# Loading K and V of two heads per transfer in a one-token attention kernel

## The chip, the cores and the metric

The kernel runs on one core of a Trainium2 chip. The metric is the device time of one execution in microseconds. Three timed executions of the kernel before took 524.91, 525.25 and 526.60 us; their median, 525.25 us, is the number that the changed kernel is measured against. The engines are called by their short names: PE is TensorE (PEld its weight loads), DVE is VectorE, ACT is ScalarE, POOL is GpSimd, SP is the engine that issues the DMAs here.

## What is computed

One token passes through two attention layers and two small mixer layers, in turn, with the same weights and the same K and V caches both times:

```python
x = A_x                                                   # (1, 1, 640)
x = x + _A_ref(_layernorm(x), A_k_cache, A_v_cache, A_wq, A_wo)
x = x + _B_ref(_layernorm(x), B_w1, B_w2, B_w3, B_w4)
x = x + _A_ref(_layernorm(x), A_k_cache, A_v_cache, A_wq, A_wo)
x = x + _B_ref(_layernorm(x), B_w1, B_w2, B_w3, B_w4)

def _A_ref(x, k_cache, v_cache, wq, wo):                  # 32 heads, Dh = 192
    W = 4096                                              # the last 4096 of 32768 keys
    q = (x @ wq) split into heads
    k, v = k_cache[:, :, Sk - W:, :], v_cache[:, :, Sk - W:, :]
    p = softmax(einsum("bhqd,bhkd->bhqk", q, k) * Dh ** -0.5)
    return (einsum("bhqk,bhkd->bhqd", p, v) joined over heads) @ wo
```

`_B_ref` is a layer norm, a gelu MLP of 640 to 1536 to 640, and a residual. (A part of it multiplies rows shifted in time; with one row it adds nothing, and the kernel leaves it out.) One head's K is 4096 x 192 bf16 numbers, 1.573 MB, and so is its V. Read twice for 32 heads, K and V make up nearly all the data that the kernel moves.

## The kernel before

**Data and cells.** K of a head lies in HBM as 4096 rows of 192 numbers. One DMA (`load_k`, L130) puts it into a cell of on-chip memory: partition p of the 128 gets keys 32p to 32p + 31, which are 12,288 contiguous bytes. V is loaded in the same way (`load_v`, L143). There are 11 cells of 12,288 bytes per partition (`NCELL`, L74). `take` (L114) hands out the cell that has been free longest, `give` (L119) returns it. Weights wo, w3 and w4 live in cells too. K of seven heads (`NKEEP`) stays on chip in transposed form between the two attention layers; two V heads and a part of a third are kept as well.

**The order of loads.** `layer_stream` (L203 on) writes down the order of all loads for a layer, and `need` issues them in that order on SP as the program asks for them. The instructions themselves may run long before: SP issues a load as soon as its cell is free, and a limited number of loads may be in flight. All engines but POOL run in the order in which the program was written (`manual_schedule`).

**Scores.** The matmul needs the 192 head dimensions on partitions. `transpose_quart` (L358) turns a quarter of a head's K with one DVE transpose in blocks of 32 x 32 words of 4 bytes (L375, 768 words per partition), four times a head. The target is a cell called the area, one head large, whose quarters are reused in turn. `scores` (L441) then runs 24 matmuls a head (L451, 256 columns each) for one head; the head's query stands in `Qblk` in a block form. Scores of four heads share one PSUM tile.

**Softmax.** Heads are treated in eight groups of four. `softmax_steps` (L471) has the steps part_max (DVE, L476), turn_max (PE, L481), full_max (DVE, L486 and L491), spread_max (PE L499, then ACT's exp, L505), turn_p (DVE, L510), swap (16 small PE matmuls with the constant `Eq`, L521, and an ACT copy to `PT`, L524), recip.

**PV and the fold.** `pv` (L558) multiplies a head's probabilities with V in 16 matmuls of 384 columns (L567): two key rows at once, a weight of two columns. The sum is in `O_ps`, of which there is one. A DVE transpose (L574) brings it to `o_sb`; `o_fold` (L576) sums it over partitions with small matmuls. `out_proj` or `out_row` multiply with wo.

**The order of work in a group.** The loop at L732 works on group `cur` while it prepares the scores of the next, `nxt`. It first runs the softmax of `cur`, interleaved with the transposes and scores of the first head of `nxt` (L764 to L799). Then for each head of `cur` it runs `pv`, then the transposes and scores of another head of `nxt` (L838 to L842), then `o_fold`. In the last two groups (`hurry`, `final`) the scores are pulled forward and the softmax of the last group is run early. Layer 0 goes through the groups from head 31 down to 0, layer 1 from 0 up.

**The end.** After the last V come wo of the last two groups in pieces, w3 and w4 in halves; the mixer of layer 1 works on each as it lands (L860 on), and a row of 640 numbers is stored.

Of the kernel before, what the change touches and what calls it, by code (L numbers as in the profile page):

```python
# [17 lines left out]
P = 128  # L18
# [17 lines left out]
def kernel(  # L36
# [26 lines left out]
    QH = 4  # L63
# [12 lines left out]
    NKEEP, NCELL = 7, 11  # L76
# [13 lines left out]
    cells = ctx.enter_context(tc.tile_pool(name="cells", bufs=1))  # L90
# [15 lines left out]
    kx = const.tile([P, VN], BF16, name="kx")  # L106

# [3 lines left out]
    free = deque(range(NCELL))  # L111
    cell_of = {}

    def take(key):  # L114
        i = free.popleft()
        cell_of[key] = i
        return cells.tile([P, FREE], BF16, tag=f"cell{i}", name=f"cell{i}")

    def give(key):  # L119
        free.append(cell_of.pop(key))  # L120
# [11 lines left out]

    def load_v(layer, h):
        t = take(("v", layer, h))
        src = A_v_cache[0, h, s0:Sk, :].rearrange("(p j) d -> p (j d)", p=P)
        cut = (2 * VW,) if h == VP else (FREE - VN,) if h == VX else ()
        if layer == 1 and h in GROUPS[layer][-1][-2:]:
            cut = FREE // 2,
        i = 0
        for e in cut + (FREE,):  # L140
            kept_v = h == VP or h == VX and i > 0
            if layer == 0 or not kept_v:
                nc.sync.dma_start(v_pair(t, h, i, e - i), src[:, i:e])  # L143
            i = e
        return t
# [55 lines left out]
    LOADERS = {"x": load_x, "k": load_k, "v": load_v, "wq": load_wq, "wo": load_wo, "w3": load_w3, "w4": load_w4}  # L201

    def layer_stream(layer):  # L203
# [14 lines left out]

        if layer == 0:
            for hh in groups[0]:  # L220
                k_item(hh)
        for gi, cur in enumerate(groups):
            nxt = list(groups[gi + 1]) if gi + 1 < len(groups) else []
            late = gi + 2 >= len(groups)
            for i, hh in enumerate(cur):
                if nxt:
                    k_item(nxt.pop(0))
                if nxt and late and i == 2:
                    k_item(nxt.pop(0))
                v_item(hh)  # L230
                if later and seq[-1] == ("k", layer, NKEEP):
                    seq.append(later.pop())
                if layer == 0 and gi + 1 == len(groups) and i < 2:
                    seq.append(("wo", layer, groups[gi + i - 1][0] // QH))
            if gi + 2 < len(groups) and gi >= layer:
                seq.append(("wo", layer, cur[0] // QH))
# [25 lines left out]
    ones = const.tile([P, P], F32, name="ones")  # L262
    nc.vector.memset(ones[:], 1.0)
# [13 lines left out]
    even = const.tile([P, 1], F32, name="even")  # L277
    nc.vector.reduce_sum(even[:], ident[:].rearrange("p (m two) -> p m two", two=2)[:, :, 0], axis=AX.X)
    lo = const.tile([P, 1], F32, name="lo")
    nc.vector.reduce_sum(lo[:], ident[:, 0:64], axis=AX.X)  # L280
    maskq = const.tile([P, 4], F32, name="maskq")
    nc.vector.tensor_tensor(out=maskq[:, 0:1], in0=lo[:], in1=even[:], op=ALU.mult)
    nc.vector.tensor_tensor(out=maskq[:, 1:2], in0=lo[:], in1=maskq[:, 0:1], op=ALU.subtract)
    nc.vector.tensor_tensor(out=maskq[:, 2:3], in0=even[:], in1=maskq[:, 0:1], op=ALU.subtract)
    nc.vector.tensor_scalar(out=maskq[:, 3:4], in0=lo[:], scalar1=-1.0, scalar2=1.0, op0=ALU.mult, op1=ALU.add)
# [6 lines left out]
    eps1 = const.tile([P, 1], F32, name="eps1")  # L292
    nc.vector.memset(eps1[:], eps)
# [26 lines left out]
    def ln_center(x, rowsum):  # L320

        mean_ps = psm.tile([P, 1], F32, tag="psm")
        nc.tensor.matmul(mean_ps[:], lhsT=ones[:], rhs=rowsum[:, 0:1], start=True, stop=True)
# [10 lines left out]
        def total():  # L334
            var_ps = psm.tile([P, 1], F32, tag="psm")
            nc.tensor.matmul(var_ps[:], lhsT=ones[:], rhs=ssq[:, 0:1], start=True, stop=True)
            return var_ps
# [20 lines left out]
    def transpose_quart(layer, h, q):  # L358
# [17 lines left out]
        if q == NT - 1:  # L376
            give(("k", layer, h))
        return T
# [62 lines left out]
    def scores(h, Ts, q0, ST_ps, hq):  # L441

        ng = NGK // NT
        Q = Qblk[:, h // QH % 2, hq * QHEAD:(hq + 1) * QHEAD].rearrange("p (f x) -> p f x", x=QW)
        views = [T.rearrange("p (g f i t) -> p g f i t", f=NFB, g=ng, i=P) for T in Ts]
        for f in range(NFB):
            for t in range(2):
                n = 2 * f + t
                for i, T4 in enumerate(views):
                    r = 32 * (q0 + i)  # L450
                    nc.tensor.matmul(  # L451
                        ST_ps[r:r + QW, :].rearrange("p (g i) -> p g i", g=ng), lhsT=Q[:, n, :],
                        rhs=T4[:, :, f, :, t],
                        start=(hq == 0 and n == 0), stop=(hq == QH - 1 and n == NCOL - 1))
# [16 lines left out]
    def softmax_steps(n, ST_ps, sc):  # L471
# [25 lines left out]
        def spread_max():  # L497
            nb_ps = psm.tile([P, 1], F32, tag="psm")
            nc.tensor.matmul(nb_ps[:], lhsT=held["w"],  # L499
                             rhs=ones[0:1, 0:1], start=True, stop=True)  # L500
# [13 lines left out]

        def swap():
            ng = NGK // NT
# [6 lines left out]
            PT = big.tile([P, n, NJ4 * NGK], BF16, name="PT")  # L523
            nc.scalar.copy(PT[:].rearrange("p h c -> p (h c)"), PT_ps[:].rearrange("p h j g -> p (h j g)"))  # L524
            l_ps = psm.tile([P, QH], F32, tag="psm")
            nc.tensor.matmul(l_ps[:], lhsT=ones[:], rhs=held["lh"][:], start=True, stop=True)  # L526
            held["lps"] = l_ps
            return PT
# [28 lines left out]

    def pv(layer, h, hq, PT, mid=None):  # L558
# [17 lines left out]
    def o_fold(h, oT, rl, add=False):  # L576
        r = slice(32 * (h % QH), 32 * (h % QH) + 32)
        oT_ps = psm.tile([P, NA], F32, tag="psm")
        if not add:
            for e in range(2):  # L580
                nc.tensor.matmul(oT_ps[r, :], lhsT=Lq[:], rhs=o_sb[:, e, :, e], start=(e == 0), stop=(e == 1))  # L581
# [3 lines left out]
        nc.vector.tensor_add(o2[:], o_sb[:, 0, :, 0], o_sb[:, 1, :, 1])  # L585
# [53 lines left out]
    def attention(layer, x_cur, rs_cur, x_new, z_new, rs_new, ss_new):  # L639
# [5 lines left out]
        last_plain = [h for g in groups for h in g if h >= NKEEP][-1]  # L645
# [3 lines left out]
        def softmax_scale():  # L649
            rstd = power(total()[:, 0:1], 1.0 / D, eps1[:], "rstd")  # L650
# [6 lines left out]

        def S(h, half, ST_ps, hq):
            if layer == 1 and h < NKEEP:
                if half == 1:  # L660
                    scores(h, [Th.pop((h, q)) for q in range(NT)], 0, ST_ps, hq)
                    give(("T", h))
                return
            scores(h, [Th.pop((h, q)) for q in (2 * half, 2 * half + 1)], 2 * half, ST_ps, hq)
            if half == 1 and layer == 0 and h == last_plain:
                give(("area", layer))
                area[0] = None

        def add_y(y_ps, n):
            y_new = x_new if n == 0 else sm.tile([P, ND], F32, name="y_acc")  # L670
            if n == 1:
# [5 lines left out]
                def center():  # L677
                    nm_ps = psm.tile([P, 1], F32, tag="psm")
                    nc.tensor.matmul(nm_ps[:], lhsT=ones[:], rhs=rs[:, 0:1], start=True, stop=True)
# [25 lines left out]
        for hq, h in enumerate(groups[0]):  # L705
            for half in range(2):
                if layer == 0:
                    T(h, half)
                else:
                    Th.update({(h, q): transpose_quart(layer, h, q) for q in (2 * half, 2 * half + 1)})  # L710
                S(h, half, ST, hq)
                if (hq, half) == (0, layer):
                    qb[2]()
                    qb[3]()
# [17 lines left out]
        for gi, cur in enumerate(groups):  # L732
            nxt = list(enumerate(groups[gi + 1])) if gi + 1 < len(groups) else []
            ST_n = None
            if nxt:
                part_max, turn_max, full_max, spread_max, turn_p, swap, recip = softmax_steps(len(cur), ST, sc)
                ST_n = next_scores()
                if layer == 1 and gi == 0:
# [7 lines left out]
                    for q2, h2 in keep:  # L746
                        for half in range(2):
                            T(h2, half)
                            S(h2, half, ST_n, q2)
# [10 lines left out]
                else:  # L760
# [3 lines left out]
                    h0 = nxt[0][1]  # L764
                    T(h0, 0)
                    part_max()
                    T(h0, 1)
                    S(h0, 0, ST_n, 0)
                    turn_max()
                    full_max()  # L770
                    S(h0, 1, ST_n, 0)
                    spread_max()
                    h1 = nxt[1][1]
# [9 lines left out]
                    T(h1, 0)  # L783
# [12 lines left out]
                    T(h1, 1)  # L796
# [3 lines left out]
                    nxt.pop(0)  # L800
# [7 lines left out]
            if layer == 1 and gi == 0:  # L808
                order.insert(0, order.pop(cur.index(VC)))
            for hq, h in order:  # L810
                pv(layer, h, hq, PT, fold)
                if final:
# [5 lines left out]
                    if hq < QH - 2:  # L818
                        o_fold(h, oT, rl)
                    else:  # L820
                        def fold(h=h):
                            o_fold(h, oT, rl)

                    continue
                if hurry and hq == 1:
                    (q2, h2), (q3, h3) = nxt
                    for half in range(2):
                        T(h2, half)
                        S(h2, half, ST_n, q2)
                    T(h3, 0)  # L830
                    S(h3, 0, ST_n, q3)
                    T(h3, 1)
                elif hurry and hq == 2:
                    S(h3, 1, ST_n, q3)
                    steps = softmax_steps(len(cur), ST_n, sc)
                    steps[0]()
                    steps[1]()
                elif nxt and not (hurry and hq == 3):  # L838
                    q2, h2 = nxt.pop(0)
                    for half in range(2):  # L840
                        T(h2, half)
                        S(h2, half, ST_n, q2)  # L842
                o_fold(h, oT, rl, len(groups) - 4 > gi >= 2 * layer)
# [14 lines left out]
    def mixer(layer, x_cur, z, rs_cur, ss_cur, x_new, rs_new):  # L858
# [5 lines left out]
        nc.tensor.matmul(s1_ps[:], lhsT=ones[:], rhs=rs_cur[:, 0:1], start=True, stop=True)  # L864
        s2_ps = psm.tile([P, 1], F32, tag="psm")
        nc.tensor.matmul(s2_ps[:], lhsT=ones[:], rhs=ss_cur[:, 0:1], start=True, stop=True)
# [119 lines left out]
```

## Time and profile before

| What | Value |
|---|---|
| median of three runs | 525.25 us |
| the profiled execution: span from first to last instruction | 522.9 us |
| its own time beyond the span | not given |
| HBM read | 216.47 MB, 414 GB/s over the span |
| PE busy | 330.3 us (63%), 4146 matmuls |
| DVE busy | 294.6 us (56%), 589 instructions |
| ACT busy | 49.5 us (9%) |
| mean granted TensorE clock | 0.675 of full |
| one K or V load | 1536 KB; in steady state 26 to 31 us from issue to landing, since several wait in the queue |

Some groups of instructions, by shape:

```profile
L574 DVE STREAM_TRANSPOSE o_sb<-O_ps 128x384 f32<-128x384 f32 x64 | 37.2, 582 | 112.4 <-PE O_ps L567 112.3
...
L375 DVE STREAM_TRANSPOSE cell_277<-cell_1403 128x768 uint32<-128x768 uint32 x4 | 3.7, 956 | 0.1
```

Each row names the line, the engine and operation, output and input with shapes and count; then busy us and mean ns of one; then how long the engine stood idle just before, and for whom. A busy share is an average over the whole run. The rows of the page that show the DMA engines, and the chain of waits, are in the prediction; both say what happens where, which a busy share doesn't.

### The profile page before, as it was taken

The numbers are of one execution on the slowest core, as the hardware profiler recorded it, in microseconds if no ns is written. First come the engines' busy times: TensorE is split into PE (matmuls) and PEld (weight loads), VectorE is DVE, ScalarE is ACT, GpSimd is POOL, SyncE is SP. The second block draws the span as 40 slices with busy tenths as digits, with TensorE's granted clock in tenths as the row PEclk, the third lists the DMA queues.
The fourth block names the chain that finished last, engine by engine and source line by source line (L and its number), as shares of the span: only waits on it lengthen the run. The fifth ranks groups of instructions, "written<-read, shape, count | busy, mean of one in ns | idle before, by whom it ended". The sixth has DMA issues, their size and how long they took to land.

```text
span 522.9 us, 9589 instructions
## 1 busy us (share of the span) xinstructions
PE 330.3 (63%) x4146; PEld 195.5 (37%) x4146; DVE 294.6 (56%) x589; ACT 49.5 (9%) x175; POOL 4.0 (1%) x16
## 2 busy tenths in 40 slices
PE   2057668666665566767655866667675666647675
PEld 2023334333332333434333544334343333425344
DVE  2067656666574664556624264766576866654722
ACT  1000101010010100001011101001010101001011
POOL 2000000000000000000000000000000000000000
PEclk9995656567677776576555567657787865766755
DMA  8999999999999999999999999999999999999996
GB/s 345 429 424 425 423 426 427 423 424 423 427 421 428 424 422 428 423 423 423 423 399 398 388 425 427 424 424 423 426 423 424 426 423 426 421 427 425 420 410 237
DMA packets 23949, 217.08 MB, mean 415 GB/s; under 512 B 2532, under 2 KB 3044, under 8 KB 8420
## 3 DMA queue, kind: packets, MB, share of 16 engines
q1 hardware_dynamic: 23908, 216.48, 99.0%
q8 instruction: 32, 0.52, 0.4%
q14 instruction: 9, 0.07, 0.0%
HBM read 216.47 MB, written 0.00 MB: 414 GB/s over the span
## 4 chain that ended last, share of the span: by engine, by line
DMA 43%; PE 27%; DVE 25%; issue 2%; ACT 2%; SPq 1%; DVEq 0%; ACTq 0%
PE ST_ps L451 11%; DVE cell_3304 L375 9%; PE O_ps L567 8%; DVE cell_277 L375 8%; DMA cell_1925<-in_A_k_cache_dram 6%; DMA cell_4933<-in_A_k_cache_dram 5%; DMA cell_1629<-in_A_k_cache_dram 5%; DMA cell_1329<-in_A_k_cache_dram 5%; DMA cell_4637<-in_A_k_cache_dram 5%; DMA cell_5324<-in_A_v_cache_dram 5%; DMA cell_275<-in_A_k_cache_dram 4%; DVE o_sb L574 2%; DMA cell_2478<-in_A_v_cache_dram 2%; DMA cell_2690<-in_A_v_cache_dram 2%; DMA cell_5423<-in_B_w_dram 2%
## 5 line engine op out<-in xcount | busy, mean ns | idle before, releaser
L451 PEld LDWEIGHTS <-Qblk 128*16 128x16 bf16 x1536 | 86.1, 113 | 178.6 <-issue 151.1
L451 PE MATMUL ST_ps<-cell_277,Qblk 128*16 128x256 bf16 x600 | 70.1, 392 | 50.9 <-DVE cell_277 L375 34.3
L574 DVE STREAM_TRANSPOSE o_sb<-O_ps 128x384 f32<-128x384 f32 x64 | 37.2, 582 | 112.4 <-PE O_ps L567 112.3
L451 PE MATMUL ST_ps<-cell_3304,Qblk 128*16 128x256 bf16 x600 | 67.3, 382 | 43.5 <-DVE cell_3304 L375 28.3
L567 PEld LDWEIGHTS <-PT 128*2 128x2 bf16 x1024 | 47.2, 102 | 21.8 <-issue 11.3
L510 DVE STREAM_TRANSPOSE o_sb<-o_sb 128x256 bf16<-128x256 bf16 x16 | 7.1, 445 | 34.1 <-ACT o_sb L505 25.0
L582 ACT ACTIVATE oT<-oT_ps,rl 32x6 bf16<-32x6 f32 x40 | 10.3, 258 | 163.5 <-PE oT_ps L581 157.1
L581 PEld LDWEIGHTS oT_ps<-o_sb,Lq 128*32 128x32 f32 x160 | 13.2, 145 | 19.9 <-issue 16.1
L581 PE MATMUL oT_ps<-o_sb,Lq 128*32 128x6 f32 x160 | 13.9, 196 | 10.4 <-DVE o_sb L574 9.9
L587 ACT ACTIVATE oT<-oT_ps,rl 32x6 bf16<-32x6 f32 x24 | 6.2, 258 | 108.4 <-PE ST_ps L451 93.7
L405 PE MATMUL qT_ps<-xc,wq_sb 128*128 128x1 bf16 x210 | 7.2, 165 | 13.4 <-DMA wq_sb<-in_A_wq_dram 12.5
L419 DVE TENSOR_TENSOR Xq<-qT_ps,maskq 128x24 bf16<-128x24 f32 (+1 forms) x18 | 2.8, 157 | 18.3 <-PE qT_ps L405 18.3
L521 PE MATMUL PT_ps<-o_sb,Eq 128*32 128x32 bf16 x256 | 7.2, 237 | 9.2 <-DVE o_sb L510 4.0
L394 PE MATMUL qr_ps<-wq_sb,xc 128*1 128x384 bf16 x90 | 12.8, 433 | 0.0
L521 PEld LDWEIGHTS <-Eq 128*32 128x32 bf16 x256 | 5.5, 111 | 18.9 <-issue 18.8
L405 PEld LDWEIGHTS <-wq_sb 128*128 128x128 bf16 x210 | 6.8, 104 | 14.8 <-DMA wq_sb<-in_A_wq_dram 13.6
L502 ACT COPY nb_sb<-nb_ps 128x1 f32<-128x1 f32 x16 | 2.5, 159 | 97.6 <-PE nb_ps L499 97.6
L526 PE MATMUL l_ps<-lh,ones 128*128 128x4 f32 x32 | 8.5, 336 | 4.9 <-ACT PT L524 4.9
L499 PEld LDWEIGHTS nb_ps<-ones,o_sb 1*128 1x128 f32 x32 | 7.6, 292 | 7.4 <-issue 5.5
L526 PEld LDWEIGHTS l_ps<-lh,ones 128*128 128x128 f32 x32 | 7.1, 275 | 7.5 <-ACT PT L524 7.1
L499 PE MATMUL nb_ps<-ones,o_sb 1*128 1x1 f32 x32 | 8.9, 345 | 1.5 <-DVE o_sb L491 1.5
L426 PE MATMUL Qrep_ps<-Xq,Lb 128*128 128x24 bf16 (+1 forms) x18 | 3.2, 179 | 10.4 <-DVE Xq L419 10.1
(376 smaller groups left out, 533.2 us busy)
## 6 DMA issues: line engine op xcount, KB each, us to landing
wq_sb<-in_A_wq_dram SPq DMA_DIRECT2D x5, 1536.0 KB, 12.7
cell_275<-in_A_k_cache_dram SPq DMA_DIRECT2D x1, 1536.0 KB
cell_309<-in_A_k_cache_dram SPq DMA_DIRECT2D x1, 1536.0 KB, 26.4
cell_346<-in_A_k_cache_dram SPq DMA_DIRECT2D x1, 1536.0 KB, 27.1
cell_376<-in_A_k_cache_dram SPq DMA_DIRECT2D x1, 1536.0 KB
cell_444<-in_A_k_cache_dram SPq DMA_DIRECT2D x1, 1536.0 KB, 30.8
cell_503<-in_A_v_cache_dram SPq DMA_DIRECT2D x1, 1536.0 KB, 30.8
cell_505<-in_A_k_cache_dram SPq DMA_DIRECT2D x1, 1536.0 KB, 30.8
```

Source lines behind the costliest of these rows:

```text
L375: nc.vector.transpose(Tu, Ku[:, :, q * NY:(q + 1) * NY])
L394: nc.tensor.matmul(qr_ps[32 * i:32 * i + 1, :], lhsT=xc[:, kc:kc + 1], rhs=wq_sb[:, kc, t0 * P + i * N:t0 * P + (i + 1) * N], start=(kc == ...
L405: nc.tensor.matmul(qT_ps[:, tl:tl + 1], lhsT=wq_sb[:, kc, t * P:(t + 1) * P], rhs=xc[:, kc:kc + 1], start=(kc == 0), stop=(kc == ND - 1))
L451: nc.tensor.matmul(ST_ps[r:r + QW, :].rearrange("p (g i) -> p g i", g=ng), lhsT=Q[:, n, :], rhs=T4[:, :, f, :, t], start=(hq == 0 and n == ...
L499: nc.tensor.matmul(nb_ps[:], lhsT=held["w"], rhs=ones[0:1, 0:1], start=True, stop=True)
L510: nc.vector.transpose(held["PrT"], held["Pr"])
L521: nc.tensor.matmul(PT_ps[32 * m:32 * (m + 1), :, :, ng * q:ng * (q + 1)], lhsT=Eq[:, q, :], rhs=src[:, m:QW:NM], start=True, stop=True)
L526: nc.tensor.matmul(l_ps[:], lhsT=ones[:], rhs=held["lh"][:], start=True, stop=True)
L567: nc.tensor.matmul(O_ps[r:r + 2, :], lhsT=PT[:, hq, 2 * i:2 * i + 2], rhs=v_pair(V, h, 2 * i * Dh, 2 * Dh), start=(i < 4), stop=(i >= NB - 4))
L574: nc.vector.transpose(o_sb[:], O_ps.rearrange("p (e a c) -> p e c a", e=2, c=NA))
L581: nc.tensor.matmul(oT_ps[r, :], lhsT=Lq[:], rhs=o_sb[:, e, :, e], start=(e == 0), stop=(e == 1))
L582: nc.scalar.activation(oT[r, :], oT_ps[r, :], ACTF.Copy, scale=rl[r, 0:1])
```

## The change

Heads are taken in pairs where possible: heads 8 to 31 in layer 0 and 20 to 31 in layer 1. The others are handled as before (`NSINGLE`). For a pair,

- one DMA loads K of both heads, and one V of both. Partition 2r + h gets keys 64r to 64r + 63 of head h: 24,576 contiguous bytes per partition, two cells side by side. The last V pair of layer 1 comes in two halves.
- the transposed area of a pair has two cells. A quarter takes three transposes (one for each 64 of the head dimensions) of 512 words, which separate the two heads on the way: they write words that are 3,072 bytes apart in turn.
- scores of a head keep their 24 matmuls of 256 columns.
- P is turned by 32 small matmuls, half with `Eq` and half with a second constant `Eqs` with neighbours exchanged, and two ACT copies, each with a mask for even or odd partitions.
- `pv_pair` runs 32 matmuls for two heads, with a weight of four columns that is zero where a partition belongs to the other head; then one transpose to `o_sb` for both.
- the loop of a group works in steps of half a pair: both quarters of a half, then the scores of both heads.

The cells become parts of one tile, `arena`, and a written list, `plan`, says for each `take` which cell it gets. The constant `ones` becomes one column that is broadcast, and four small constants move into one tile.

The diff, cut to its core:

```diff
-    NKEEP, NCELL = 7, 11
+    NKEEP, NCELL, NSINGLE = 7, 11, (8, 20)
...
+    arena = const.tile([P, NCELL * FREE], BF16, name="arena")
...
-    free = deque(range(NCELL))
+    free = set(range(NCELL))
...
+    plan = deque([
+        0, 2, 4, 6, 8, 0, 4, 10, 6, 0, 8, 4, 10, 0, 8, 6, 4, 10, 8, 0, 6, 4, 10, 8, 0, 6, 4, 0, 10,
...
+    ])
+
+    def is_pair(layer, h):
+        return h >= NSINGLE[layer]
+
+    def take(key, n=1):
+
+        i = plan.popleft()
+        for c in range(i, i + n):
+            free.remove(c)
+        cell_of[key] = range(i, i + n)
+        return arena[:, i * FREE:(i + n) * FREE]
...
+    def pair_rows(cache, h):
+        return cache[0, h:h + 2, s0:Sk, :].rearrange("h (r j) d -> r h (j d)", r=P // 2)
+
+    def load_kk(layer, h):
+        t = take(("kk", layer, h), 2)
+        nc.sync.dma_start(t, pair_rows(A_k_cache, h))
+        return t
+
+    def load_vv(layer, h):
+        t = take(("vv", layer, h), 2)
+        src = pair_rows(A_v_cache, h)
+        n = FREE if (layer, h) == (1, H - 2) else 2 * FREE
+        for i in range(0, 2 * FREE, n):
+            nc.sync.dma_start(t[:, i:i + n], src[:, :, i:i + n])
+        return t
...
-        if layer == 1 and h in GROUPS[layer][-1][-2:]:
-            cut = FREE // 2,
...
-    ones = const.tile([P, P], F32, name="ones")
-    nc.vector.memset(ones[:], 1.0)
+    cols = const.tile([P, 5], F32, name="cols")
+    one, even, odd, lo, eps1 = (cols[:, i:i + 1] for i in range(5))
+    nc.vector.memset(one, 1.0)
+    ones = one.broadcast_to([P, P])
...
+    def transpose_pair(layer, h, q):
+
+        Kn = need("kk", layer, h)
+        if area[0] is None:
+            area[0] = take(("area", layer), 2)
+        T = area[0][:, 2 * q * QUART:2 * (q + 1) * QUART]
+        nj = 2 * NJ4 * NGK // NT
+        Ku = Kn.bitcast(U32).rearrange("p (q j f b) -> p q f j b", q=NT, j=nj, f=NFB)[:, q]
+        Tu = T.bitcast(U32).rearrange("p (c f j r e) -> p f j e r c", c=2, f=NFB, j=nj // 2, e=2)
+        for f in range(NFB):
+            nc.vector.transpose(Tu[:, f], Ku[:, f])
+        if q == NT - 1:
+            give(("kk", layer, h))
+        return T
...
+        def swap_pair():
+            nb = SW // 32
+            PT_ps = psm.tile([P, 2, n, NT, nb], F32, tag="psm")
+            src = held["PrT"].rearrange("p (b i) -> p i b", i=32)
+            for m in range(NM):
+                for q in range(NT):
+                    for e, E in enumerate((Eq, Eqs)):
+                        nc.tensor.matmul(PT_ps[32 * m:32 * (m + 1), e, :, q], lhsT=E[:, q, :],
+                                         rhs=src[:, m:QW:NM], start=True, stop=True)
+            PT = big.tile([P, 2 * n * NJ4 * NGK], BF16, name="PT")
+            for c, side in enumerate((even, odd)):
+                nc.scalar.activation(
+                    PT[:].rearrange("p (h b c e) -> p e h b c", h=n // 2, c=2, e=2)[:, :, :, :, c],
+                    PT_ps[:].rearrange("p e (h c) q b -> p e h c (q b)", c=2)[:, :, :, c], ACTF.Copy, scale=side)
+            return PT
...
+    def pv_pair(layer, h, hq, PT, mid=None):
+        V = need("vv", layer, h)
+        NB = NJ4 * NGK
+        lhs = PT[:].rearrange("p (h b m) -> p h b m", b=NB, m=4)
+        for i in range(NB):
+            if mid is not None and i == NB // 2:
+                mid()
+            r = 32 * (i % 4)
+            nc.tensor.matmul(O_ps[r:r + 4, :], lhsT=lhs[:, hq // 2, i, :],
+                             rhs=V[:, 2 * i * Dh:2 * (i + 1) * Dh], start=(i < 4), stop=(i >= NB - 4))
+        give(("vv", layer, h))
+        nc.vector.transpose(o_sb[:], O_ps.rearrange("p (e a c) -> p e c a", e=2, c=NA))
...
+            if is_pair(layer, cur[0]):
...
+                    if hq == 0 and nxt_pair:
+                        (_, _, sa, sb, _), (ta, tb, sa2, sb2, _), (tc, td, sc2, sd2, _) = todo
+                        todo = []
+                        sa()
+                        sb()
+                        ta()
+                        tb()
+                        pv_pair(layer, h, hq, PT)
+                        sa2()
+                        sb2()
+                        fold()
+                        tc()
+                        td()
+                        sc2()
+                        sd2()
+                        if hurry:
+                            steps = softmax_steps(layer, groups[gi + 1], ST_n, sc)
+                            steps[0]()
+                            steps[1]()
+                        continue
+                    pv_pair(layer, h, hq, PT)
+                    if todo and hq == 0:
+                        whole(todo.pop(0))
+                    fold()
+                    if todo:
+                        whole(todo.pop(0))
```

Here `ta`, `tb` are the two quarters of a half pair, and `sa`, `sb` the scores of its two heads. In a softmax part of a group, before this, the first half pair of `nxt` goes around part_max and full_max, and the quarters of its second half go around turn_p and swap, in the places where single heads had theirs.

## The prediction

> **What bounds the kernel now.** I read the page's DMA rows first, then the chain of waits in order of time, then busy time by stretch, then the groups of instructions by shape.
>
> The DMA rows of the page:
>
> ```profile
> DMA  8999999999999999999999999999999999999996
> GB/s 345 429 424 425 423 426 427 423 424 423 427 421 428 424 422 428 423 423 423 423 399 398 388 425 427 424 424 423 426 423 424 426 423 426 421 427 425 420 410 237
> DMA packets 23949, 217.08 MB, mean 415 GB/s; under 512 B 2532, under 2 KB 3044, under 8 KB 8420
> ...
> q1 hardware_dynamic: 23908, 216.48, 99.0%
> ```
>
> The transfers never pause between the first slice and the last, so the time is start-up plus bytes over rate plus a tail. The rate is about 424 GB/s while K and V load, and falls to 388-399 in the three slices around the layer boundary, where rows of weights are short. That points at a cost per packet.
>
> The chain of waits:
>
> ```profile
> 76.73 1.75 DVE cell_277 L375 x2
> ...
> 107.03 1.75 DVE cell_277 L375 x2
> ...
> 110.85 26.70 DMA cell_1329<-in_A_k_cache_dram
> ...
> 141.68 27.72 DMA cell_1629<-in_A_k_cache_dram
> ...
> 505.28 10.63 DMA cell_5423<-in_B_w_dram
> ```
>
> Until 110.85 us the chain is TensorE and VectorE catching up; one group of four heads took 107.03 - 76.73 = 30.3 us. Afterwards each group waits for its K. A group's bytes are 8 x 1.573 + 0.983 = 13.57 MB, at 424 GB/s 32.0 us. So compute has only 1.7 us to spare in a group. The last link is the second half of w3.
>
> Busy time by stretch (one catching-up group, one waiting group, the last K/V stretch):
>
> ```profile
> 76.00:107.00 31.00, 21.14 (x218) 11.42 (x218) 20.23 (x39) 3.06 (x10) 0.00 (x0) 0.56 1.01 424
> ...
> 138.00:170.00 32.00, 19.59 (x218) 11.14 (x218) 19.90 (x37) 3.06 (x10) 0.00 (x0) 0.72 1.01 425
> ...
> 481.00:505.00 24.00, 16.91 (x214) 10.33 (x210) 12.12 (x23) 2.63 (x10) 0.00 (x0) 0.64 1.01 420
> ```
>
> No engine is near full (columns: PE, PEld, DVE, ACT, POOL, clock, DMA share, GB/s); the 30 us are alternation of VectorE and TensorE. Packets of the queue in two stretches, 400-420 us (almost all K and V) and 500-510 us (short weight rows):
>
> ```profile
> q1 hardware_dynamic: 778, 8.48, 100.4%
> ...
> q1 hardware_dynamic: 1064, 4.06, 101.3%
> ```
>
> [...] Per engine, 20,000 ns = 530,000 B x + 48.6 c and 10,000 ns = 253,750 B x + 66.5 c give c = 9.8 ns and 27.1 B/ns; with the stretch 280-290 us (1449 packets, 3.84 MB) instead, c = 13.7 ns. I take 12, ends 10 and 14. [...]
>
> **The change part by part.**
>
> *Fewer packets.* 35 transfers of 24,576 B rows replace 70 of 12,288 B rows; each has 128 row packets and 16 small completion packets (the "under 512 B" count, 2532, is 16 for each of some 157 transfers). That removes 35 x 144 = 5040. The last V pair goes from four half loads to two: 2 x 144 = 288. Sum 5328, or 333 per engine; x 12 ns = 4.0 us, ends 3.3 and 4.7. No byte is saved: the same seven K and the same V are kept. [...] SP issues fewer DMAs; it is not late now.
>
> *Transposes.* Per pair of heads, 8 transposes of 768 words become 12 of 512. A run of four took 3.51 us (L375), 0.877 a piece[...]. A pair's transposes go from 8 x 0.877 = 7.0 to 12 x 0.61 = 7.3 us. The new output is written one word in 3,072 B, then steps of 8 B. No row shows such a write. [...] I take nothing: L574 reads PSUM at 24 B steps, 384 words in 0.582 us, against 0.541 for L556, which reads PSUM straight. That is a read, not a write, so both ends stay.
>
> *TensorE.* Scores stay at 24 matmuls a head, PV at 32 for two heads; same columns. The turn of P goes from 16 to 32 matmuls (+0.45 us, one L521 burst) and two copies of 0.27 instead of one (+0.27), both before PV. Two of four PV-to-o_sb round trips vanish (o_sb 0.58 each).
>
> *A group, worked through with the durations of the group 76.7-107.0.* T for one quarter is 3 x 0.61 = 1.83. Two quarters and the max: scores begin at 4.1 (2.2 before). They now wait for both quarters, and behind them on TensorE stand the max's transpose, the second scores and the row work, so the whole softmax chain is 1.9 us later. Second scores end at 7.2, exp at 8.7, turn 9.1, third quarter 11.0, adds 12.0, fourth quarter 13.9, PT ready 13.6. Scores (24 x 0.12 = 2.9) to 17.0; PV (32 x 0.087 = 2.8) to 19.8; o_sb 20.4; meanwhile transposes of the second pair end at 18.2. Its scores to 22.7; last transposes 20.6 to 24.3, scores to 27.2, PV to 30.0, o_sb and adds 30.75. So 30.75 us against a DMA period of 32.0 - 0.4 = 31.6 (4 pair loads x 144/16 x 12 ns = 0.43). The cover holds by 0.8 us, and [...] (22 scores in 1.68 us when unstalled, 0.076 each), which would give near 28.5.
>
> *Cells.* The area takes two cells, so nine are left: four pairs and wo. A K pair for the group after next now goes into the cell of the V pair that PV frees at 19.8 after the K landed. That transfer is due at 31.6 - 7.3 = 24.3: 4.5 us to spare instead of the 26-30 us of queue before. A wait there holds up everything behind it on SP's queue. First K lands 3.7 us later (3.1 MB instead of 1.6), and the first groups are late by that: in the second group I find the cell free at 98.8 us and wanted at 97.8, 1 us of idle DMA at most. I count 0, bound 1.
>
> *Tail.* Last group: its first K pair lands 36.6 us before the last V; the same walk, with the row turn (2.2 us, L635) and one more softmax, puts z (the residual sum at L688 that the last mixer starts from) 45.0 to 49.5 us after that landing[...], so 8.4 to 12.9 after the last V. Before it was 512.38 - 505.27 = 7.1, and the second half of w3 left 1.15 us of slack. Loss 0.15 to 4.6; I take 1.0[...].
>
> *Rest* (one column for ones, odd mask, Eqs): some 0.5 us before the first K lands, hidden by wq's load.
>
> Sum against the profiled execution: span 522.9 - 4.0 + 1.0 = 519.9. The median of 525.25 stands 2.35 above that span, which I take as what lies around it: 522.3.
>
> **Rivals.**
> 1. Forecast: DMA stays the bound, 522.3. For: 99% DMA share, packet cost fitted twice. Against: 0.8 us of cover. Own range 519 to 524.5. Chance 0.58.
> 2. Gain eaten by late compute: [...] (+4.6 instead of 1.0) gives 522.3 + 3.6 = 525.9, half of that excess 524.1; named time 525.9. For: the last group is on the critical side already. Chance 0.17.
> 3. Slower: VectorE becomes the bound through the strided writes, in nine pair groups. Of 24 pieces in a group 18 lie on the path. It decides from 0.8 / 18 = 0.045 us extra a piece. [...] Named time 537. [...] against: L574. Chance 0.13.
> 4. Two heads 12.6 MB apart in HBM, or coarse cells, hold the DMA back: 1.5 us in each of nine groups, +13.5, 535.8. For: 4.5 us of lead; against: each row is longer than now. Chance 0.12.
>
> **How the numbers follow.** About 0.3% (1.6 us) can be told from no change. Faster by more (under 523.7): 0.55 of case 1 and 0.04 of 2, together 0.59. Same: 0.03 + 0.10 of these and 0.02 of 4, together 0.15. Slower (over 526.8): 0.03 of 2, all of 3, 0.10 of 4, together 0.26. The range 519 to 533 leaves out case 3, the larger half of 4 and a sliver below: about 0.2. Its lower end allows 5 us of packet savings and no lost tail, its upper end 1.2 us lost in each of nine groups.
>
> **What would show it.** Right: about 18,600 packets, 429-430 GB/s in pair stretches, transposes at 0.61 us pitch, chain still on DMA. Wrong: transposes above 0.65 us, idle DMA slices at 80-250 us with SP waiting for PE, z more than 8.3 us behind the last V.

## The result, and the profile after

The changed kernel takes 568.76 us (median, 564.54 to 570.44) against 525.08 us for the kernel before, measured beside it: ratio 1.082, 95% interval 1.078 to 1.086. It is slower by 43.7 us; the forecast was 522.3 us, 3 us faster, with a range up to 533. The profiled execution, one of 568.38 us, has a span of 565.6 us.

The page of the changed kernel: span, engines, DMA rows, shares of the chain, and the groups of its two kinds of transposes (busy us and mean ns of one, then the engine's idle time ahead of them):

```profile
span 565.6 us, 9860 instructions
...
PE 342.4 (61%) x4290; PEld 202.3 (36%) x4290; DVE 359.4 (64%) x646; ACT 54.5 (10%) x184; POOL 4.0 (1%) x16
...
DMA  8999756989999996999999999999999989898793
...
DMA packets 18623, 217.10 MB, mean 384 GB/s; under 512 B 1940, under 2 KB 2452, under 8 KB 7316
...
DVE 47%; PE 30%; DMA 16%; issue 4%; ACT 3%; SPq 1%; DVEq 0%; ACTq 0%
...
L433 DVE STREAM_TRANSPOSE arena<-arena 128x512 uint32<-128x512 uint32 x216 | 206.8, 1077 | 10.8 <-DMA arena<-in_A_k_cache_dram 10.6
...
L418 DVE STREAM_TRANSPOSE arena<-arena 128x768 uint32<-128x768 uint32 x84 | 75.2, 943 | 2.7 <-DMA arena<-in_A_k_cache_dram 2.5
```

Packets are as forecast (18,623), and so are the bytes. Those under 512 B fall from 2532 to 1940, by 592 = 37 x 16 for 37 transfers fewer: a pair's load has 16 of them, as a single one has. But the DMA row, a line of nines before, has holes at 57-99 us, at 113-127 us (a shallow one), at 212-226 us, and several from 452 us on, and VectorE heads the chain with 47%. L418 is the old transpose of 768 words, at 943 ns much as before (956 in the row above). L433, the new one of 512 words, takes longer than it: 1077 ns. (A piece lasts longer than the step from one start to the next, which is what the forecast speaks of: 1077 ns against 0.94 us below.)

The chain in order of time (start, us, what), one pair group of layer 0:

```profile
128.12 2.90 DVE arena L433 x3
...
131.23 2.84 DVE arena L433 x3
...
138.36 2.83 DVE arena L433 x3
...
145.59 5.63 DVE arena L433 x6
...
162.88 2.82 DVE arena L433 x3
```

From one group to the next are 162.88 - 128.12 = 34.8 us; the loads of a group need 31.6 (13.57 MB at 430 GB/s). The transposes follow one another on the path, three at a time, at 0.94 us each (six in 5.63), where the forecast had 0.61. No link between these is a DMA.

Stretches of the changed kernel (PE, PEld, DVE, ACT, POOL busy; granted TensorE clock, DMA share, GB/s):

```profile
70.00:100.00 30.00, 17.06 (x206) 9.97 (x202) 25.19 (x38) 3.09 (x10) 0.00 (x0) 0.74 0.59 239
160.00:190.00 30.00, 18.35 (x200) 10.38 (x192) 24.62 (x40) 3.61 (x11) 0.00 (x0) 0.66 1.01 430
```

Where the queue is fed (160-190 us), it moves 430 GB/s, what the forecast said of it. At 70-100 us 41% of the DMA time is missing. The waits of SP's queue show why (total us over the run, times, longest), first the changed kernel, then the run e1_dense_write of the next section, which differs in the order of the written words alone:

```profile
SPq L159 <- DVE arena L433: 39.9, 4, 13.7
SPq L151 <- DVE arena L433: 38.2, 5, 12.3
```

```profile
SPq L159 <- DVE arena L433: 27.4, 4, 9.6
SPq L151 <- DVE arena L433: 23.8, 5, 7.9
```

The V and K loads of pairs (L159, L151) wait for cells that late transposes still read, as often as in e1 and longer in sum. SP waits for a cell in any of these kernels; it costs time where nothing is left in flight meanwhile, as at 70-100 us (DMA share 0.59, against 1.01 at 160-190 us).

How the loss builds up is seen from the start of the softmax maximum (L547, once in each group of four heads) on VectorE's timeline, here beside the run e3_heads_adjacent, which differs in the place of the transposed words and, with it, in the step of the reads:

| group (in order of time) | 1 | 2 | 3 | 4 | 5 | 6 | 7 | 8 | 9-12 | 13 | 14 | 15 | 16 |
|---|---|---|---|---|---|---|---|---|---|---|---|---|---|
| changed kernel, us | 67.6 | 100.2 | 135.0 | 169.7 | 204.4 | 235.3 | 264.1 | 289.1 | 329.3-406.7 | 439.7 | 479.7 | 512.9 | 543.0 |
| e3, us | 57.8 | 83.9 | 115.4 | 147.2 | 178.8 | 205.6 | 239.0 | 264.0 | 304.0-381.0 | 412.7 | 445.2 | 477.4 | 500.6 |
| behind, us | 9.8 | 16.4 | 19.7 | 22.5 | 25.6 | 29.8 | 25.1 | 25.1 | 25.1-25.7 | 26.9 | 34.6 | 35.5 | 42.4 |

Nearly all of it is lost in the nine groups of pairs (1-6 and 14-16, whose first transposes lie in the group ahead, so that group 13 already loses 1.2 us). Groups 7 to 12, all of single heads, lose next to nothing (0.6 us), and get back 4.7 us at group 7.

### The profile page after: what moved, and what is told of

Read it like the earlier page. It is cut to its first block, busy times and chain, and to the rows that moved or that the text cites. A ratio compares the mean times of both kernels' runs of the same rounds, so it can differ in the third digit from the quotient of the medians.

```text
span 565.6 us, 9860 instructions
## 1 busy us (share of the span) xinstructions
PE 342.4 (61%) x4290; PEld 202.3 (36%) x4290; DVE 359.4 (64%) x646; ACT 54.5 (10%) x184; POOL 4.0 (1%) x16
## 2 busy tenths in 40 slices
DMA packets 18623, 217.10 MB, mean 384 GB/s; under 512 B 1940, under 2 KB 2452, under 8 KB 7316
## 4 chain that ended last, share of the span: by engine, by line
DVE 47%; PE 30%; DMA 16%; issue 4%; ACT 3%; SPq 1%; DVEq 0%; ACTq 0%
DVE arena L433 31%; PE ST_ps L511 11%; DMA arena<-in_A_k_cache_dram 11%; DVE arena L418 8%; PE O_ps L665 5%; PE O_ps L651 5%; DMA arena<-in_A_v_cache_dram 4%; ACT o_sb L566 1%; PE nb_ps L560 1%; DVE o_sb L654 1%; DVE o_sb L672 1%; DVE o_sb L571 1%; PE PT_ps L583 1%; PE l_ps L598 1%; PE y_ps L734 1%
## 5 line engine op out<-in xcount | busy, mean ns | idle before, releaser
L511 PE MATMUL ST_ps<-arena,Qblk 128*16 128x256 bf16 x1536 | 173.7, 372 | 133.7 <-DVE arena L433 74.4
L433 DVE STREAM_TRANSPOSE arena<-arena 128x512 uint32<-128x512 uint32 x216 | 206.8, 1077 | 10.8 <-DMA arena<-in_A_k_cache_dram 10.6
L418 DVE STREAM_TRANSPOSE arena<-arena 128x768 uint32<-128x768 uint32 x84 | 75.2, 943 | 2.7 <-DMA arena<-in_A_k_cache_dram 2.5
L651 PE MATMUL O_ps<-arena,PT 128*4 128x384 bf16 x576 | 53.0, 470 | 0.6 <-ACT PT L587 0.4
L672 DVE STREAM_TRANSPOSE o_sb<-O_ps 128x384 f32<-128x384 f32 x28 | 16.2, 580 | 50.5 <-PE O_ps L665 50.5
L665 PE MATMUL O_ps<-arena,PT 128*2 128x384 bf16 x442 | 42.6, 459 | 7.5 <-DMA arena<-in_A_v_cache_dram 7.5
L654 DVE STREAM_TRANSPOSE o_sb<-O_ps 128x384 f32<-128x384 f32 x18 | 10.3, 574 | 36.7 <-PE O_ps L651 36.7
L651 PEld LDWEIGHTS <-PT 128*4 128x4 bf16 x576 | 27.2, 110 | 13.1 <-issue 4.6
L681 ACT ACTIVATE oT<-oT_ps,rl 32x6 bf16<-32x6 f32 x40 | 10.3, 257 | 163.2 <-PE oT_ps L680 162.9
L665 PEld LDWEIGHTS <-PT 128*2 128x2 bf16 x448 | 18.5, 98 | 14.5 <-issue 7.8
L598 PE MATMUL l_ps<-lh,cols 128*128 128x4 f32 x32 | 8.6, 339 | 8.5 <-ACT PT L587 6.5
L583 PEld LDWEIGHTS <-Eq 128*32 128x32 bf16 x144 | 9.8, 114 | 8.1 <-issue 8.1
```

The lines of the kernel that those rows point to most:

```text
L418: nc.vector.transpose(Tu, Ku[:, :, q * NY:(q + 1) * NY])
L433: nc.vector.transpose(Tu[:, f], Ku[:, f])
L511: nc.tensor.matmul(ST_ps[r:r + QW, :] if is_pair(layer, h) else ST_ps[r:r + QW, :].rearrange("p (g i) -> p g i", i=P), lhsT=Q[:, n, :], rh ...
L583: nc.tensor.matmul(PT_ps[32 * m:32 * (m + 1), e, :, q], lhsT=E[:, q, :], rhs=src[:, m:QW:NM], start=True, stop=True)
L598: nc.tensor.matmul(l_ps[:], lhsT=ones, rhs=held["lh"][:], start=True, stop=True)
L651: nc.tensor.matmul(O_ps[r:r + 4, :], lhsT=lhs[:, hq // 2, i, :], rhs=V[:, 2 * i * Dh:2 * (i + 1) * Dh], start=(i < 4), stop=(i >= NB - 4))
```

## Experiments on the transposes

Three theories were tried. A: the strided writes make each piece longer, and VectorE becomes the bound. B: coarse cells, HBM places or the later softmax hold the loads back, and the slow pieces only fill waiting time. C: more and smaller instructions cost it.

**Dense writes, nothing else.** e1_dense_write:

```diff
-        Tu = T.bitcast(U32).rearrange("p (c f j r e) -> p f j e r c", c=2, f=NFB, j=nj // 2, e=2)
+        Tu = T.bitcast(U32).rearrange("p (f j e r c) -> p f j e r c", c=2, f=NFB, j=nj // 2, e=2)
```

> Changed kernel with one edit: the 512-word transposes of a pair write their words densely, one block of 32 words after the other; the reads of the scores stay as they are, so the scores of a pair mix keys of both heads. Theory A (writing words 3,072 B apart in turn costs VectorE about 0.31 us a piece, and 18 of 24 pieces of a group lie on the path in nine groups): pieces at 0.61-0.65 us instead of 0.95, group period 31-32 us, 521-527 us. Theory B (coarse cells, rows of two heads in HBM, or the later softmax hold the transfers back; the slow pieces are covered): pieces get faster, but the group period stays over 33 us and the time over 540. Theory C (36% more words in more pieces, whatever they write): pieces at 0.8 or more, over 545.

Measured: 526.35 us, ratio 1.0019 (1.0008 to 1.0030). Its page, and its chain by time:

```profile
DMA  8999999999999999989999999999999999999995
...
L433 DVE STREAM_TRANSPOSE arena<-arena 128x512 uint32<-128x512 uint32 x216 | 133.6, 677 | 41.0 <-DMA arena<-in_A_k_cache_dram 40.8
```

```profile
95.57 13.37 DMA arena<-in_A_k_cache_dram
...
116.94 1.80 DVE arena L433 x3
...
126.73 13.82 DMA arena<-in_A_k_cache_dram
```

Same instructions and same count, 677 ns instead of 1077; three in 1.80 us are 0.60 each. The row of nines is back, and each group's chain leads through a K load again (13.37 and 13.82 us are two such loads, from the free cell to the landing). VectorE stands idle for 40.8 us in all ahead of these pieces until K lands, where it was 10.6. One line of address order is worth 42.4 us. B and C fall as causes of the loss.

**Dense writes with the heads taken apart by the reads.** e2_dense_read8 has e1's write, and:

```diff
-            views = [T.rearrange("p (c f i t) -> p c f i t", c=2, f=NFB, t=2)[:, h % 2] for T in Ts]
+            views = [T.rearrange("p (f i c t) -> p c f i t", c=2, f=NFB, t=2)[:, h % 2] for T in Ts]
...
-            nc.scalar.activation(out=Pr, in_=ST_ps, func=ACTF.Exp,
+            pair = is_pair(layer, group[0])
+            nc.scalar.activation(out=Pr.rearrange("p (j r e) -> p j e r", r=16, e=2) if pair else Pr,
+                                 in_=ST_ps.rearrange("p (j e r) -> p j e r", r=16, e=2) if pair else ST_ps, func=ACTF.Exp,
```

> Dense writes as in e1_dense_write, and the scores read one head's words at a step of 8 B out of the dense rows; the exp writes its columns in an order that puts the words back in place. Computes what the reference does. Theory A: as e1, 521-527 us, if the step of 8 B costs TensorE nothing; at a doubled score matmul (24 x 4 x about 0.08 = 7.7 us a group) 570 or more. Theory B: over 540. Theory C: over 545.

Measured: 527.66 us, ratio 1.0045 (1.0030 to 1.0060), 677 ns a piece. The score matmuls don't double at a step of 8 B, which by the estimate above would have meant 570 us or more; what the step costs them is shown further below, on e3.

**The heads side by side.** e3_heads_adjacent, with e2's view for the reads and no change of the exp:

```diff
-        Tu = T.bitcast(U32).rearrange("p (c f j r e) -> p f j e r c", c=2, f=NFB, j=nj // 2, e=2)
+        Tu = T.bitcast(U32).rearrange("p (f j r e c) -> p f j e r c", c=2, f=NFB, j=nj // 2, e=2)
```

> The two words of two heads that follow each other are written side by side (8 B), then a step of 16 B; the scores read at a step of 8 B in the right order. Computes what the reference does. [...] Theory A with a price only for the far step of 3,072 B: 0.61-0.65 us, 521-527. Theory B: over 540 in any case.

Measured: 527.10 us, ratio 1.0036 (1.0020 to 1.0051).

```profile
L433 DVE STREAM_TRANSPOSE arena<-arena 128x512 uint32<-128x512 uint32 x216 | 133.9, 680 | 32.0 <-DMA arena<-in_A_k_cache_dram 31.7
```

Not dense (8 B, then a gap of 8 B), and still at the dense pace. This looked like a price for the far step only; the next three runs bear on that.

**The far step, with the gap inside a head closed.** e4_far_dense (with e2's exp; from here on, only the line that takes the place of the changed kernel's):

```diff
+        Tu = T.bitcast(U32).rearrange("p (c f j e r) -> p f j e r c", c=2, f=NFB, j=nj // 2, e=2)
```

> The heads stay 3,072 B apart, as in the changed kernel, but the words of a head follow each other without the gap of 4 B (the exp puts the columns in order again). Computes what the reference does. Theory A with a price for the far step: pieces at 0.93 as in the changed kernel, 565-570. [...] Theory B: over 540.

Measured: 565.16 us, ratio 1.076 (1.073 to 1.079).

```profile
L433 DVE STREAM_TRANSPOSE arena<-arena 128x512 uint32<-128x512 uint32 x216 | 202.2, 1049 | 7.7 <-DMA arena<-in_A_k_cache_dram 7.6
```

Almost the full price (1049), although each 16 B now receives four words of one head in the end. So it counts which write follows which, not how many words each 16 B have in the end.

**Nearer heads.** e5_heads_128B and e6_heads_1KB (the reads follow the order):

```diff
+        Tu = T.bitcast(U32).rearrange("p (f j c r e) -> p f j e r c", c=2, f=NFB, j=nj // 2, e=2)
...
+        Tu = T.bitcast(U32).rearrange("p (f c j r e) -> p f j e r c", c=2, f=NFB, j=nj // 2, e=2)
```

> Each run of 64 words of a transposed pair holds 32 words of one head, then 32 of the other: the words written in turn are 128 B apart instead of 3,072 B, with the gap of 4 B inside a head as in the changed kernel; the scores read runs of 32 columns at the step of 4 B that they had. If any alternation between distant lines costs: pieces 0.9 us or more, 560-570. If only a far step costs: 0.60 us a piece; the scores cost as before (11 in 1.44 us), so about as e1_dense_write: 525-527.

> The heads alternate 1,024 B apart (per 64 of the head dimensions one block of words of each head); the scores read 256 columns at a step of 4 B. A price that grows with the distance: between 0.60 and 0.92 us a piece, 530-560. A price with a threshold below 1 KB: 0.92, 560-570. A threshold above it: 0.60, 525-527.

Measured: 570.22 us, ratio 1.086 (1.083 to 1.090), and 566.78 us, 1.080 (1.078 to 1.082). The group of e5:

```profile
L433 DVE STREAM_TRANSPOSE arena<-arena 128x512 uint32<-128x512 uint32 x216 | 207.0, 1079 | 8.8 <-DMA arena<-in_A_k_cache_dram 8.6
```

1079 ns at 128 B, 1078 at 1,024 B, 1077 at 3,072 B: from 128 B on, distance has no part in it. The guess after e3 was wrong.

**A step of 8 B and one of 16 B, always forward.** e8_step_8B and e9_step_16B (the reads follow here too):

```diff
+        Tu = T.bitcast(U32).rearrange("p (f j r c e) -> p f j e r c", c=2, f=NFB, j=nj // 2, e=2)
...
+        Tu = T.bitcast(U32).rearrange("p (f g i m) -> p f g m i", f=NFB, g=nj // 4, m=4)
```

> The words that one 32-word row of a transposed block writes in turn lie 8 B apart, always forward (two of them in each 16 B); between them lie the words of the next block. The scores read two columns side by side, then a step of 16 B. [...] If they must be adjacent (8 B as one): 0.92 us a piece, 565-570.

> As e8_step_8B with a step of 16 B: [...]always forward, nothing alternates. The columns of P stay in the order of the reads, so weights of the pairs meet rows of V of other keys. [...] If it is for jumping back and forth between two places: 0.60, 525-528.

Measured: 528.97 us, ratio 1.0056 (1.0037 to 1.0075), and 568.36 us, 1.082 (1.079 to 1.085). The groups of e8 and of e9:

```profile
L433 DVE STREAM_TRANSPOSE arena<-arena 128x512 uint32<-128x512 uint32 x216 | 133.8, 679 | 32.7 <-DMA arena<-in_A_k_cache_dram 32.5
```

```profile
L433 DVE STREAM_TRANSPOSE arena<-arena 128x512 uint32<-128x512 uint32 x216 | 205.8, 1069 | 8.7 <-DMA arena<-in_A_k_cache_dram 8.5
```

679 against 1069 ns: at a step of 8 B a piece keeps the dense pace (677 in e1), so two words need not be adjacent; at a step of 16 B it pays what the changed kernel pays (1077), and going back and forth is not needed for it. Together with e3 (steps of 4 and 12 B, 680 ns) and e5 (back and forth over 128 B, 1079): rows whose words follow each other at 12 B or less were written at the dense pace, those with 16 B or more from each word to the next were not. In e1, e3 and e8 at least two words in a row also fall into the same aligned 16 B, and in e9 only one; whether that or the step alone decides, these runs don't tell apart. The price is 0.94 - 0.60 = 0.34 us in 512 words (the changed kernel against e1), when pieces follow one another.

## Experiments on the rest of the forecast

With the writes mended, e3 is still 2 us slower than the kernel before, where the forecast had 3 us less. Its DMA share shows two holes (70-80 and 230-240 us, columns as above):

```profile
70.00:80.00 10.00, 7.34 (x90) 3.84 (x83) 6.28 (x14) 1.03 (x4) 0.00 (x0) 1.00 0.87 346
230.00:240.00 10.00, 7.48 (x73) 3.57 (x65) 8.34 (x12) 0.52 (x2) 0.00 (x0) 0.50 0.81 318
```

They are worth 1.3 and 1.9 us. e1, whose scores read at a step of 4 B, has in the first stretch:

```profile
70.00:80.00 10.00, 4.45 (x66) 2.77 (x66) 7.37 (x15) 1.00 (x4) 0.00 (x0) 0.92 0.97 396
```

A share of 0.97 against 0.87: the slower reads of the scores (last section) may have a part in the first hole. In the second hole, SP's queue issues nothing between these two loads (start, us, what):

```profile
223.90 0.33 SPq L170 DMA_DIRECT2D arena<-in_A_v_cache_dram  x1
...
236.68 0.33 SPq L143 DMA_DIRECT2D arena<-in_A_k_cache_dram  x1
```

The K of head 1 of layer 0 waits there for a cell that the plan gives it while the area of head 7 still lies in it. e7_adjacent_cell gives it another (in the plan):

```diff
-        8, 9, 1, 6, 10, 2, 3, 4, 4, 9, 6, 7, 10, 4, 5, 3, 0, 6, 9, 4, 10, 3, 0, 9, 10, 3, 0, 9, 10,
+        8, 9, 1, 6, 10, 2, 3, 4, 4, 9, 6, 7, 10, 0, 5, 3, 4, 6, 9, 4, 10, 3, 0, 9, 10, 3, 0, 9, 10,
```

> e3_heads_adjacent with two entries of the written plan exchanged: the K of head 1 of layer 0 goes into the cell that a wo left long before, the K of head 2 into the one that it had (the rest is as there). What is left of theory B: the trace of e1 and e3 shows 2.0 us of missing DMA share at 230-240 us, while the queue waits 10 us with this K for a cell. If that is a loss of the end: 525.0-525.5 (2 us less than e3). If something later takes it up (the idle DMA is not what sets the end): within 0.5 us of e3's 527.1.

Measured: 525.99 us, ratio 1.0018 (1.0008 to 1.0028): 1.1 us less than e3, in between. The hole at 230-240 us is gone (share 1.01), but the one at 70-80 us was deeper in this execution, 0.78. e10_two_cells mends that too, by exchanging 0 with 8 and 1 with 9 in the plan from its tenth entry on, so that a V pair of the second group takes a cell that a V pair has left, and not the one of a K pair that is still being transposed:

```diff
-        0, 2, 4, 6, 8, 0, 4, 10, 6, 0, 8, 4, 10, 0, 8, 6, 4, 10, 8, 0, 6, 4, 10, 8, 0, 6, 4, 0, 10,
+        0, 2, 4, 6, 8, 0, 4, 10, 6, 8, 0, 4, 10, 8, 0, 6, 4, 10, 0, 8, 6, 4, 10, 0, 8, 6, 4, 8, 10,
...
```

> e7_adjacent_cell with one more change of the plan: cells 0-1 and 8-9 exchanged from the second group's first V pair on, so that this V pair takes the cell that a V pair has left (free at about 71 us in e3) and not the one of a K pair whose transposes end at 74.4 us. e3 lost 1.3 us of DMA share at 70-80 us there, e7 2.2. If that is a loss of the end: 524.0-524.8, same as or a little under the kernel before. If not: within 0.5 us of e7's 526.0.

Measured: 524.12 us, ratio 0.9984 (0.9974 to 0.9993). This is the fastest version, 0.9 us (0.16%) under the kernel before. Its two stretches, and the end of its chain:

```profile
70.00:80.00 10.00, 7.74 (x98) 4.14 (x91) 6.02 (x15) 0.81 (x4) 0.00 (x0) 1.00 1.01 429
230.00:240.00 10.00, 7.19 (x75) 4.10 (x76) 8.19 (x12) 0.80 (x4) 0.00 (x0) 0.67 1.01 417
```

```profile
506.37 11.40 DMA arena<-in_B_w_dram
...
517.82 0.84 PE y_ps L1113 x25
```

No hole is left in either, and weights that load end the chain, with no late softmax ahead of them. So the late softmax that the forecast feared at the end costs nothing here.

e11_short_rows puts the old row length back into e10:

```diff
-        nc.sync.dma_start(t, pair_rows(A_k_cache, h))
+        src = pair_rows(A_k_cache, h)
+        for i in range(0, 2 * FREE, FREE):
+            nc.sync.dma_start(t[:, i:i + FREE], src[:, :, i:i + FREE])
...
-        n = FREE if (layer, h) == (1, H - 2) else 2 * FREE
+        n = FREE
```

> e10_two_cells with each K and V pair of heads loaded in two transfers with rows of 12,288 B instead of one with rows of 24,576 B (the first half of each row, then the second; places and cells as there). It undoes the first step of the prediction alone: 35 transfers more, 5,040 packets more in the queue (18,580 to about 23,620). At 12 ns a packet over 16 engines the end comes 3.8 us later: 527.9. At the 7.6 ns that the rates of 424.7 and 428.7 GB/s at 100-220 us (before, e1) give: 2.4 us later, 526.5. If the transfers' rows do not set the end: within 0.5 us of e10's 524.1.

Measured: 526.71 us, ratio 1.0035 (1.0021 to 1.0048), 2.6 us more than e10. The load queue's packets, MB and share, then those of e10:

```profile
q1 hardware_dynamic: 23620, 216.48, 98.6%
```

```profile
q1 hardware_dynamic: 18580, 216.48, 98.6%
```

5,040 packets more over 16 engines are 315 each; 2.6 us / 315 = 8.2 ns. The queue's share is the same in both, in spans of 524.6 and 521.6 us, so the added time is time at work and not a hole. The saving by fewer packets exists, and is smaller than forecast. The intervals of the two ratios, taken together, allow 1.8 to 3.5 us, which is 5.7 to 11.1 ns; 12 ns lies outside. (What the 35 transfers more may cost beside their packets is in the figure.)

## Why the prediction was wrong

*The step that failed* is in "Transposes", on the strided writes: "I take nothing". An upper end was left open beside it, which was the author's estimate; the runs show +0.34 us a piece. The reason given was L574, which reads PSUM at 24 B steps for almost nothing (0.582 us against 0.541). That row is a read of another memory; nothing in it spoke of a write to SBUF. The 0.61 us for the dense piece, the author's estimate too, was right (0.60 in e1), and the bytes, packets and the rate of 430 GB/s were too.

*Rival 3* was the right mechanism, with a chance of 0.13. Its named time of 537 us rested on a price a piece that was the author's estimate. Its reckoning, 18 pieces at the price, less the cover of 0.8 us, in nine groups, gives with the measured 0.34 us (18 x 0.34 - 0.8) x 9 = +48 us; e1 against the changed kernel gives 42.4. That the two are near is luck, since two of its terms were wrong and offset each other. The first is the cover of 0.8 us. e3's second group, whose chain holds no wait for a load, takes 83.9 - 57.8 = 26.1 us from maximum to maximum, not 30.75, which leaves 31.6 - 26.1 = 5.5 us. VectorE's waits for K in e3's next groups say nearly the same (start, us, what, and the idle time ahead of it):

```profile
110.36 1.90 DVE L433 STREAM_TRANSPOSE arena<-arena 128x512 uint32<-128x512 uint32 x3 [4.32 <-DMA arena<-in_A_k_cache_dram]
...
142.23 1.90 DVE L433 STREAM_TRANSPOSE arena<-arena 128x512 uint32<-128x512 uint32 x3 [4.66 <-DMA arena<-in_A_k_cache_dram]
...
173.78 1.90 DVE L433 STREAM_TRANSPOSE arena<-arena 128x512 uint32<-128x512 uint32 x3 [4.62 <-DMA arena<-in_A_k_cache_dram]
```

With the shorter wait for each group's second K pair (0.56, 0.42 and 0.22 us) these are 4.8 to 5.1 us. The second term is the 18 pieces: the changed kernel's 34.8 us are 8.7 more than 26.1, as much as all 24 pieces at 0.34 (8.2). The granted clock differs between the two (0.83 in e3 at 57.8-83.9 us, 0.66 in the changed kernel at 128.1-162.9 us), so how the 8.7 divide into pieces and clock stays open. The loss isn't the same nine times either. By the table above it is 2.8 to 4.2 us in groups 3 to 6, where 24 pieces less the cover would be 8.2 - 5 = 3.2, and 6.6 to 9.8 us in the first two groups, at group 14 and at group 16. At group 15 it is 0.9 us; why so little there was not looked into.

*The 28.5 us* that the walk through a group also names rest on 22 scores in 1.68 us. Two stretches of the kernel before, one around 12 scores that take 1.45 us (from 78.84 us on) and one in that burst (from 89.37 us on), have the same granted clock, 0.50:

```profile
78.80:82.10 3.30, 3.25 (x26) 1.76 (x25) 2.29 (x4) 0.00 (x0) 0.00 (x0) 0.50 0.99 417
89.40:91.00 1.60, 1.60 (x33) 1.26 (x31) 0.75 (x2) 0.00 (x0) 0.00 (x0) 0.50 1.00 422
```

So the quicker pace there is not one of a higher clock; what makes it was not tried.

*Fewer packets*: 4.0 us forecast; 8.2 ns instead of 12 makes it 2.7 for the 333 packets of an engine. The two fits of before (9.8 and 13.7 ns) were made on short weight rows; for rows of 12 to 24 KB the second lies outside the 5.7 to 11.1 ns of e11, the first inside.

*Cells*: "I count 0, bound 1" was wrong by the 3.0 us that e10 gains over e3. The text did name 1 us in the second group, but at 98 us and for a K pair that waits for the cell of a V pair; the hole of e3 lies at 70-80 us, where a V pair waits for the cell of a K pair. The one at 230-240 us, between pairs and single heads, wasn't looked for.

*TensorE*: the turn of P (32 matmuls) takes 1.28 us and the two copies 0.83, against 0.9 and 0.54 worked out. Both are links of e1's chain (from 119.73 us on); what these 0.7 us cost the end was not tried.

*Tail*: 1.0 us taken; nothing is lost in e10, whose chain ends in loads.

Put right, the sum is - 2.7 for packets, + 3.0 for cells, 0 for the tail and + 42.4 for the writes: + 42.7 us against the measured + 43.7. The term for the writes is itself the difference between the changed kernel and e1, so only the rest, + 0.3, is put to a test: e1 lies 1.0 us above the kernel before. Part of the gain of packets is missing even in e10: 0.9 us under the kernel before instead of 2.7. Where the other 1.8 us go was not settled.

## What to carry to other kernels

Before a transfer is widened, follow the new order of the words through every engine that touches them: here a gain of some 2.7 us in the loads was bought with a reordering that fell to the transposes, at 42 us. For a VectorE transpose of 4-byte words into SBUF as here, look at how far apart two words lie that follow each other in the instruction's own order: if it is 16 B at every word, as in e9 (1069 ns a piece), or more, reckon with some 0.7 ns a word more (0.34 us / 512), and first try an order that puts them side by side in pairs, as in e3 (680 ns), since the reader had the gaps far cheaper here (0.44 us in 23 matmuls, next section). And where a step's cost is bounded from two sides and no row shows it, hold the ends against the cover: with the 0.8 us of cover and 18 pieces that it had worked out, anything over 0.045 us a piece decided the sign, and evidence on another memory was not enough to take zero.

## What the runs showed of the hardware

A matmul that streams 256 columns at a step of 8 B out of SBUF (e3) is slower in part than at 4 B (e1). Both after the same wait, and with a granted clock of 0.50 in that stretch, a burst of scores on TensorE's timeline (start, us), of e1, then of e3:

```profile
111.84 1.44 PE L511 MATMUL ST_ps<-arena,Qblk 128*16 128x256 bf16 x11 [0.24 <-DVE arena L433]
```

```profile
113.23 1.80 PE L511 MATMUL ST_ps<-arena,Qblk 128*16 128x256 bf16 x11 [0.23 <-DVE arena L433]
```

This burst takes 1.80 us instead of 1.44; the next, of 12 matmuls, 1.53 instead of 1.45. Why the two bursts differ was not tried. It isn't a doubling. Most of it lies under the loads here: VectorE's wait for K ahead of its pieces falls from 40.8 us (e1) to 31.7 (e3), and e3 takes 0.7 us more than e1, which their intervals don't tell apart, and e2 takes 1.3 us more.
